# Chunked attention with a top-1 expert layer on one core: transposes in halves, a second score bank, and an early candidate list

## The chip, the cores and the metric

One core of a Trainium2 chip runs the whole kernel as one program. The metric is device time in microseconds (us); the median of the runs shown is the time of the kernel. The core's engines run their own instruction streams in order and wait for each other through semaphores: PE (matrix multiply, with its weight loads listed apart as PEld), DVE (vector), ACT (scalar, activations), POOL (general) and SP, which here only issues transfers. Transfers run on 16 DMA engines.

## The reference

`q`, `k`, `v` are 8 batches x 8 heads x 576 positions x 64. Attention is local to chunks of 64 positions. Its output, 4608 tokens x 512, goes through a gate that picks one of 8 experts per token; each expert keeps the 80 tokens with the highest gate weight, and all other rows of the output are zero.

```python
scores = scale * np.matmul(q_c, k_c.transpose(0, 1, 2, 4, 3))
scores = scores - np.max(scores, axis=-1, keepdims=True)
attn = np.exp(scores)
attn = attn / (np.sum(attn, axis=-1, keepdims=True) + 1e-09)
out = np.matmul(attn, v_c)
...
logits = x @ w_gate
expert_idx = np.argmax(logits, axis=1)
...
    if len(tok_idx) > capacity:
        gw = gate_w[tok_idx]
        keep = np.argpartition(-gw, capacity)[:capacity]
        tok_idx = tok_idx[keep]
    h = np.maximum(x[tok_idx] @ w1[e], 0.0)
    out[tok_idx] = gate_w[tok_idx, None] * (h @ w2[e])
```

## The kernel before

The 4608 tokens are 36 row tiles of 128 tokens (two chunks of 64, all 8 heads); four row tiles make one group. The program's text is the order of each engine's instructions, so an instruction that waits holds up everything written after it on its engine.

A loop over row tiles (iterations 0 to 34, the 36th written out behind it) is a pipeline of depth four. Iteration i makes, in this order: the scores of tile i (`scores`, 8 matmuls into `s`, on DVE a row maximum `mx` and the difference `sm`); on every fourth iteration the gate logits of an earlier group (`gate_mm`, `gate_copy`); for tile i-1 four transposes of `sm` into `pt` and an exponential on ACT (`probs`); for tile i-2 the values matmuls into `o` and the division on DVE, which gives `x` (`values`, which also stores x to memory through POOL); in gate iterations the gate's partial sums, four transposes `lT` (`gate_sum`); for tile i-3 four transposes of x into `px`, copied by ACT (`xtrans`); then SP issues the load of tile i-2+NB (`load`: q, and keys and values in two halves into one of NB buffers `kv`, whose unused places are zeroed once at the start). `s`, `pt` and `px` have one PSUM tile each.

A gate's DVE operations, and the steps of a search for each expert's threshold, stand in two queues, from which `fill` takes up to three between two DVE operations of the loop. The search brackets the threshold from the first 16 tiles; the rest of the loop and the tail count, for 256 levels inside the bracket, how many tokens lie above each level (`signs` on ACT or `steps_` on DVE make a level tile, `tally` sums them on PE into `ph`).

Weights of the first experts (EARLY) and zero writes of the output (CLEAR) are issued on SP in late iterations. After the loop the tail gates the last eight tiles, as two chains of four tiles whose steps alternate by the string LAST, finishes the counts, takes the exact threshold (`threshold`), masks all 36 tiles, numbers the kept tokens by a running sum (`inc`, `pos`, `ptok_b`), makes a one-hot matrix for each of the 36 tiles (`hot`, on DVE, ACT and POOL), and multiplies them into a list of up to 128 candidates (`cand`). These are ranked, and the 80 best rows per expert are gathered from memory (`xgc`). Then the experts' two matmul layers run, and the results are scattered to the output.

At the program's start DVE and POOL clear the seven buffers, and 14 matmuls on a zero tile (`warm`) run on PE ahead of the first scores.

## Time and profile before

| | |
|---|---|
| median of 3 runs | 275.99 us (274.03 to 277.04) |
| the profiled execution's own time | 273.62 us |
| its span | 271.4 us |
| PE busy | 246.6 us, 91% |
| PE weight loads (PEld) | 148.9 us, 55% |
| DVE busy | 134.7 us, 50% |
| ACT busy | 77.5 us, 29% |
| POOL busy | 55.2 us, 20% |
| transfers | 84.71 MB, mean 312 GB/s |

A row of single instructions or groups gives the start (us from the span's start), the duration, the engine, the line in the kernel, the operation, the tile written and the tiles read (numbers left out), the tile mode of PE (rows*columns), the shape (partitions x elements), the type and the count; brackets hold the idle time of the engine just before and what ended it. An fp32 matmul is two records, so four transposes are counted x8, of which some records can be missing. A row of a stretch of time gives start:end, its length, then busy time and instruction count of PE, PEld, DVE, ACT and POOL, the clock that PE was granted, the busy share of the DMA engines and their rate. A row of transfers gives the count, the size of one and the median time from issue to landing.

### The profile page before, as it was taken

How to read it: one execution, taken by the hardware profiler on the slowest of the kernel's cores; microseconds unless marked ns; L12 is line 12 of the kernel's file. 1: busy time of each engine (PE TensorE's matmuls, PEld its weight loads, DVE VectorE, ACT ScalarE, POOL GpSimd, SP SyncE). 2: the span in 40 equal slices, each digit the busy share in tenths (PEclk: the TensorE clock that was granted, in tenths of full speed). 3: DMA queues.
4: the chain of work that ended last, by engine and by line, in shares of the span. 5: the costliest groups of instructions: out<-in, count | busy, mean ns of one | idle time of the engine just before them, and what ended most of it. 6: DMA issues, size and time to landing. Idle time of an engine off the chain costs nothing. (4 is left out here: it accounts for less than half of the span.)

```text
span 271.4 us, 6612 instructions
## 1 busy us (share of the span) xinstructions
PE 246.6 (91%) x2703; PEld 148.9 (55%) x2703; DVE 134.7 (50%) x419; ACT 77.5 (29%) x159; POOL 55.2 (20%) x115
## 2 busy tenths in 40 slices
PE   0579999999999999999998878999999999999970
PEld 0458777777767687787876667342343434233320
DVE  7348758686767869695873867121121112112210
ACT  1003433433443554375755330220020202001000
POOL 9020101102020203069023453500000011110011
PEclk9999999999999999999999999999999999999996
DMA  4998799989998899979999971899999999996001
GB/s 145 381 282 294 250 323 386 347 280 315 390 341 315 278 342 318 378 261 391 395 408 408 331 297 44 295 368 406 404 393 408 407 403 393 407 387 244 0 36 35
DMA packets 32755, 84.71 MB, mean 312 GB/s; under 512 B 3344, under 2 KB 3472, under 8 KB 32720
## 3 DMA queue, kind: packets, MB, share of 16 engines
q1 hardware_dynamic: 28960, 71.32, 71.6%
q0 software_dynamic: 3456, 12.32, 13.0%
q10 hardware_dynamic: 304, 0.59, 0.6%
q8 instruction: 23, 0.38, 0.6%
q14 instruction: 12, 0.10, 0.1%
HBM read 64.04 MB, written 20.45 MB: 311 GB/s over the span
## 5 line engine op out<-in xcount | busy, mean ns | idle before, releaser
L202 PE MATMUL hc<-w,xtc 128*32 128x512 f32 x384 | 44.2, 594 | 0.2 <-ACT xtc L192 0.2
L235 PE MATMUL yc<-w,htc 128*32 128x512 f32 x384 | 43.4, 593 | 0.1
L316 PE MATMUL s<-kv,q 128*64 128x128 f32 x576 | 40.0, 282 | 1.8 <-POOL capc L768 1.7
L356 PE MATMUL o<-kv,pT 128*64 128x130 f32 x576 | 39.7, 279 | 0.0
L322 DVE TENSOR_REDUCE mx<-s 128x8 f32<-128x512 f32 x36 | 24.8, 690 | 22.4 <-PE s L316 22.3
L316 PEld LDWEIGHTS s<-kv,q 128*64 128x64 f32 x576 | 31.4, 138 | 8.3 <-issue 5.8
L356 PEld LDWEIGHTS o<-kv,pT 128*64 128x64 f32 x576 | 31.1, 135 | 5.9 <-issue 5.9
L338 ACT ACTIVATE pT<-pt 128x512 f32<-128x512 f32 x36 | 21.5, 597 | 35.1 <-PE pt L336 34.8
L235 PEld LDWEIGHTS yc<-w,htc 128*32 128x32 f32 x384 | 12.5, 110 | 29.2 <-issue 28.2
L202 PEld LDWEIGHTS hc<-w,xtc 128*32 128x32 f32 x384 | 12.1, 110 | 26.0 <-issue 25.6
L367 DVE TENSOR_TENSOR x<-o,rc 128x512 f32<-128x512 f32 x36 | 24.8, 689 | 0.8 <-DMA xs<-x 0.2
L325 DVE TENSOR_TENSOR sm<-s,mx 128x512 f32<-128x512 f32 x36 | 24.8, 690 | 0.6
L389 ACT COPY xT<-px 128x512 f32<-128x512 f32 x32 | 18.6, 581 | 22.1 <-PE px L388 22.0
L336 PE MATMUL pt<-ct,sm 128*128 128x128 f32 x144 | 23.5, 286 | 0.0
L388 PE MATMUL px<-ct,x 128*128 128x128 f32 x144 | 22.7, 283 | 0.8 <-ACT kv L389 0.8
L241 POOL DMA_INDIRECT out<-ysc,si x6 | 6.0, 995 | 84.8 <-DMA out<-zero 42.4
L207 ACT ACTIVATE hsc<-hc 128x512 f32<-128x512 f32 x6 | 3.6, 598 | 64.4 <-PE hc L202 64.4
L240 DVE TENSOR_SCALAR ysc<-yc,gatec 128x512 f32<-128x512 f32 x6 | 4.5, 752 | 34.5 <-PE yc L235 34.5
L336 PEld LDWEIGHTS pt<-ct,sm 128*128 128x128 f32 x144 | 15.1, 140 | 10.2 <-issue 9.5
L388 PEld LDWEIGHTS px<-ct,x 128*128 128x128 f32 x144 | 15.4, 141 | 5.1 <-issue 4.0
L463 POOL TENSOR_TENSOR comp<-comp,ct 128x32 bf16<-128x32 bf16 x18 | 3.9, 234 | 61.0 <-DVE comp L477 61.0
L209 DVE TENSOR_SCALAR hsc<-hc 128x512 f32<-128x512 f32 x6 | 4.1, 691 | 22.9 <-PE hc L202 22.9
(160 smaller groups left out, 242.3 us busy)
## 6 DMA issues: line engine op xcount, KB each, us to landing
w<-in_w SPq DMA_DIRECT2D x12, 2048.0 KB, 20.2
kv<-in_kv SPq DMA_DIRECT2D x70, 258.0 KB, 4.9
q<-in_q SPq DMA_DIRECT2D x36, 256.0 KB, 5.3
out<-zero SPq DMA_DIRECT2D x9, 1024.0 KB, 18.2
xs<-x POOLq DMA_DIRECT2D x8, 1024.0 KB, 7.1
w<-in_w SPq DMA_DIRECT2D x8, 1024.0 KB, 8.5
xs<-x POOLq DMA_DIRECT2D x4, 256.0 KB, 8.3
kv<-in_kv ACTq DMA_DIRECT2D x2, 258.0 KB, 4.2
```

The lines of the kernel that those rows point to most:

```text
L202: nc.tensor.matmul(h[o:o + 32, :], lhsT=xT[r][:, b, o:o + 32], rhs=getw(groups[r][g])[0][:, b, 512 * f:512 * f + 512], start=(b == 0), sto ...
L235: nc.tensor.matmul(y[o:o + 32, :], lhsT=hT[r][c // 4][:, c % 4, o:o + 32], rhs=getw(groups[r][g])[1][:, c, :], start=(c == 0), stop=(c == ...
L241: nc.gpsimd.indirect_dma_start(out=out, out_offset=bass.IndirectOffsetOnAxis(ap=si[:, r:r + 1], axis=0), in_=ys, in_offset=None, bounds_ch ...
L316: nc.tensor.matmul(ps[64 * u:64 * u + 64, pr, :].rearrange("p (h k) -> p h k", h=2), lhsT=t['q'][:, pr, u, :], rhs=t['k'][:, :, pr, u, :], ...
L322: nc.vector.tensor_reduce(mx, s8, axis=AX.X, op=ALU.max)
L325: nc.vector.tensor_tensor(sm.rearrange("p c k h -> p c h k"), s8, mx[:, :, :, None].to_broadcast([P, 4, 2, 64]), op=ALU.subtract)
L336: nc.tensor.transpose(pt[:, pr, :], sv[:, pr, :], ident)
L338: nc.scalar.activation(pT, pt, AF.Exp, scale=0.125)
L356: nc.tensor.matmul(po[64 * u:64 * u + 64, pr // 2, o:o + 130].rearrange("p (h x) -> p h x", h=2), lhsT=d['pT'][:, pr, 64 * u:64 * u + 64], ...
L367: nc.vector.tensor_tensor(t['x'][:, r, :].rearrange("p (j m e) -> p j m e", j=2, m=4), pov[..., 0:64], rc[:, :, :, None].to_broadcast([P, ...
L388: nc.tensor.transpose(pm[:, pr, :], t['x'][:, r, P * pr:P * pr + P], ident)
L389: nc.scalar.copy(t['xT'][:, :, P * r:P * r + P], pm)
```

## The change

- `halves` takes the place of the four transposes of 128 by 128 in `probs` and `xtrans`: eight of 64 rows by 64 columns, the two row halves of a pair into the two banks of one tile `tp`, shared by both callers. Two further places use `tp`, `s` and `o` for the last tiles.
- `s` gets two tiles. `values` of tile 34 writes two `s` tiles in place of one of two banks, and divides each by itself.
- The gate's partial sums are four matmuls against a constant of 8 columns (`summed`) in place of four transposes and a DVE reduction; the 1e-9 of the denominator is a constant ninth column of `ex`.
- NB goes from 7 to 6, NWARM from 14 to 24, and the start is written in another order.
- For the first R1 = 24 tiles the loop takes an early threshold from the counts so far (a level that the final one can't fall below), masks, numbers and positions them (`early_steps`, queued from LEVELS at 23), and makes the one-hots 12 to 23 on POOL (`early_hot`). From iteration 26 `fill` takes one step more.
- The tail gates the last eight tiles in one chain, multiplies the first 24 tiles into `cand1`, and then masks, numbers and picks only 12 tiles and one further column, which stands for the early list. `xtrans(32)` moves ahead of `probs(35)`.

```diff
-NB = 7
+NB = 6
...
-NWARM = 14
+NWARM = 24
...
-LEVELS = {15: "l0:4 c0 c1 c2 - - - - s2 c3", 19: "l4:5 - s3 s0 c4", 23: "l5:6 s4 s1 c5",
...
+LEVELS = {15: "l0:4 c0 c1 c2 - - - - s2 c3", 19: "l4:5 - s3 s0 c4", 23: "l5:6 s4 s1 - - t",
...
-LAST = "aaabababababababababab"
...
-HALVES = 32
-HOT = 8
+HOT = 12
+R1 = 24
+R2 = RT - R1
...
+            if S.get('hurry'):
+                step_one(bounds_q)
...
         def load(i):
+            load_q(i)
+            load_kv(i)
+
+        def load_q(i):
...
+
+        def load_kv(i):
+            T, r = divmod(i, 4)
+            kb = kvb[i % NB]
             for h in range(2):
                 (nc.scalar if i < 2 and h else nc.sync).dma_start(kb[h:P:2, h], kv[T, r, h])
...
-            ps = ps1.tile([P, 4, P], F32, name=f"s{i}", tag="s")
+            ps = ps1.tile([P, 4, P], F32, name=f"s{i}", tag="s", bufs=2)
...
+        def halves(src, nm, tag="tp"):
+
+            pm = ps1.tile([P, 2, 512], F32, name=nm, tag=tag)
+            for pr in range(4):
+                for u in range(2):
+                    rows = slice(64 * u, 64 * u + 64)
+                    nc.tensor.transpose(pm[:, u, 64 * pr:64 * pr + 64], src(pr)[rows],
+                                        ident[rows, rows])
+            return pm[:, :, 0:256].rearrange("p u (a j) -> p a u j", a=4)
...
             d = U[i]
-            pt = ps1.tile([P, 4, P], F32, name=f"pt{i}", tag="pt")
             sv = d['sm'].rearrange("p c k h -> p c (k h)")
-            for pr in range(4):
-                nc.tensor.transpose(pt[:, pr, :], sv[:, pr, :], ident)
+            pt = halves(lambda pr: sv[:, pr, :], f"pt{i}")
...
-            nc.scalar.activation(pT, pt, AF.Exp, scale=0.125)
+            nc.scalar.activation(pT.rearrange("p a (u j) -> p a u j", u=2), pt, AF.Exp,
+                                 scale=0.125)
...
+        def xtrans(i, tag="tp"):
             T, r = divmod(i, 4)
             t = TT[T]
-            if pm is None:
-                pm = ps1.tile([P, 4, P], F32, name=f"px{i}", tag="m")
+            dst = t['xT'][:, :, P * r:P * r + P]
+            if tag == "s":
+                pm = ps1.tile([P, 4, P], F32, name=f"px{i}", tag="s", bufs=2)
+                for pr in range(4):
+                    nc.tensor.transpose(pm[:, pr], t['x'][:, r, P * pr:P * pr + P], ident)
+            else:
+                pm = halves(lambda pr: t['x'][:, r, P * pr:P * pr + P], f"px{i}", tag)
+                dst = dst.rearrange("p a (u j) -> p a u j", u=2)
+            nc.scalar.copy(dst, pm)
...
+        def summed(lg, lt, n):
+            for c in range(n):
+                nc.tensor.matmul(lg[:, c, :], lhsT=lt[:, P * c:P * c + P],
+                                 rhs=ct[:, C_SUM:C_SUM + NE], start=True, stop=True)
...
+            lg = ps2.tile([P, n, NE], F32, name=f"lT{rt}", tag="g")
+            summed(lg, U[rt]['lt'], n)
             gate(rt, n, lg, gates)
...
+            if rt < 28:
+                fns[3:3] = [raised]
+            else:
+                w, ws, a = each("wi", inw)
+                o, os_, b = each("wl", nlo)
...
+                fns[6:6] = [w]
+                fns[8:8] = [o, ws, os_, lambda: v.tensor_tensor(bs, g, a, op=ALU.mult),
+                            lambda: v.tensor_tensor(bs, bs, b, op=ALU.add)]
...
+            def met():
+                S['ge1'] = gk.tile([P, 2, NE], BF16, name="ge1", tag="ge")
+                nc.vector.tensor_scalar(S['ge1'], left, 0.0, None, op0=ALU.is_le)
...
+            def pos1():
...
+                places(t, mask, inc)
...
+            def ptok1():
+                S['ptok_b'] = gk.tile([P, R1], BF16, name="ptok_b", tag="ptok_b", bufs=1)
+                place_of(S['ptok_b'], S['pos1'])
...
+            q = R1 - 4
+            for fn in ((signs, (q,)), (steps_, (nc.vector, q + 1)), (signs, (q + 2,)),
+                       (steps_, (nc.vector, q + 3)), wait, wait, wait, (left_add, (q, 4)),
+                       wait, wait, wait, (met, ()), wait, wait, wait, (met_pe, ()), wait, wait,
+                       (lambda: level(thr1, S['pn1']), ()),
+                       (above, (mask, 0, R1, thr1)), (running, (inc, mask, rst1)),
+                       wait, wait, wait, wait, (pos1, ()), wait, wait, wait, (ptok1, ())):
+                bounds_q.append(fn)
...
+        def early_hot():
+            if 'ptok' in S and pool_hots:
+                hot(pool_hots.popleft(), "p", 1)
...
-            for j, kb in enumerate(kvb):
-                (nc.vector if j % 2 == 0 else nc.gpsimd).memset(kb, 0.0)
-            load(0)
+            load_q(0)
             nc.scalar.dma_start(ident, cst[:, C_ID:C_ID + P])
             warm = gk.tile([P, 2 * P], BF16, name="warm", tag="lv", bufs=LV)
             nc.vector.memset(warm, 0.0)
+            for j, kb in enumerate(kvb):
+                if j:
+                    (nc.gpsimd, nc.vector)[j % 2].memset(kb, 0.0)
+                else:
+                    nc.vector.memset(kb[:, 0], 0.0)
+                    nc.gpsimd.memset(kb[:, 1], 0.0)
+            nc.vector.memset(wgp[:, :, 8:32], 0.0)
+            load_q(1)
+            load_kv(0)
...
             warm_up(NWARM)
...
-            for n in range(1, 4):
+            load_kv(1)
+            for n in range(2, 4):
...
+            for i in range(R1 + 4, RT - 1):
+                for h in (1, 2, 3):
+                    at(i, h, early_hot)
...
+                S['hurry'] = i >= R1 + 2
...
+            xtrans(32)
...
-            xtrans(32)
-            xtrans(33, ps1.tile([P, 4, P], F32, name="px33", tag="pt"))
-            px = ps1.tile([P, 2, 4, P], F32, name="px34", tag="s")
-            xtrans(34, px[:, 0])
-            xtrans(35, px[:, 1])
-            gate_mm(28, 4)
-            gate_mm(32, 4)
-            gate_copy(28, 4)
...
-            for w in LAST:
-                step_one(tails[w])
...
-            io_h = wk.tile([P, P, HOT], BF16, name="io_h", tag="x")
...
-            tally(32, 4)
+            hot(0, "v", HOT)
+            while pool_hots:
+                early_hot()
...
+            xtrans(33)
+            xtrans(34, "s")
+            two_logits(28, ps2, "g", "a", "sm")
+            xtrans(35, "o")
+            two_logits(30, ps2, "g", "v", "sm")
...
+            lg = ps2.tile([P, 8, NE], F32, name="lT28", tag="g")
+            for rt in (28, 30, 32, 34):
+                summed(lg[:, rt - 28:], lt[rt], 2)
+            gate(28, 8, lg, gates)
+            for j in range(len(gates) - 1):
+                step_one(gates)
...
+            for rt in range(R1):
+                nc.tensor.matmul(
+                    c1.rearrange("p c e -> p (c e)"), lhsT=S[rt],
+                    rhs=comp[:, rt].rearrange("p c e -> p (c e)"),
+                    start=rt == 0, stop=rt == R1 - 1)
...
+            tally(28, 8)
+            nc.vector.tensor_reduce(
+                kc1, c1[:, 2:5, :].rearrange("p c e -> p e c"), axis=AX.X, op=ALU.add)
+            nc.scalar.copy(cand1, c1)
...
-            mask = gk.tile([P, NE, RT], BF16, name="mask", tag="mask", bufs=1)
-            nc.vector.tensor_tensor(
-                mask, keys.rearrange("p r e -> p e r"),
-                thr[:, :, None].to_broadcast([P, NE, RT]), op=ALU.is_ge)
...
+            above(mask2[:, :, 1:], R1, RT, thr)
+            nc.vector.tensor_tensor(mask2[:, :, 0], kc1, thr, op=ALU.is_ge)
+            running(inc2, mask2, rst2)
...
+            place_of(ptok2[:, 0:R2], pos2[:, :, 1:])
...
-                n = 9 - len(others)
-                hot(b0, "v", n)
-                for j, way in enumerate(others):
-                    hot(b0 + n + j, way, 1)
-                order += range(b0, b0 + 9)
...
+            cand = two[1][:, 0:5 * NE].rearrange("p (c e) -> p c e", c=5)
+            half = (R2 + NE) // 2
+            for rt in (R1, R1 + half):
+                hot(rt, "v", half)
+            for rt in range(R1, RT):
                 nc.tensor.matmul(
                     cand.rearrange("p c e -> p (c e)"), lhsT=S[rt],
-                    rhs=comp[:, rt, 0:5].rearrange("p c e -> p (c e)"),
-                    start=rt == order[0], stop=rt == order[-1])
-                if rt % 9 == 8:
-                    keep_warm(4 if rt == order[-1] else 2)
+                    rhs=comp[:, rt].rearrange("p c e -> p (c e)"),
+                    start=rt == R1, stop=False)
+            for e in range(NE):
+                nc.tensor.matmul(cand[:, :, e], lhsT=S[RT + e], rhs=cand1[:, :, e],
+                                 start=False, stop=e == NE - 1)
+            keep_warm(4)
```

`places`, `place_of`, `above` and `running` hold the matmuls, the reduction, the comparison and the scan that stood in the tail. `each` makes a product with the one-hot of the expert and its sum over the experts.

On DVE, the program's start before: `kv` are the buffers of keys and values, `warm` is what the warm-up matmuls read, `wgp` the gate's weights, `mx` the first maximum.

```order
L738 MEMSET kv_103 128x2064
L738 MEMSET kv_105 128x2064
L738 MEMSET kv_107 128x2064
L738 MEMSET kv_109 128x2064
L742 MEMSET warm 128x128
L749 MEMSET wgp 128x4x24
L322 TENSOR_REDUCE mx_184<-s_175 128x8
```

The same place after the change:

```order
L851 MEMSET warm 128x128
L856 MEMSET kv_110 128x1032
L854 MEMSET kv_111 128x2064
L854 MEMSET kv_113 128x2064
L854 MEMSET kv_115 128x2064
L858 MEMSET wgp 128x4x24
L340 TENSOR_REDUCE mx_204<-s_195 128x8
```

The memset of `warm` moved from behind four buffers to the front, the first buffer is cleared here only by half, and three whole ones follow instead of four.

On PE, a gate iteration of the loop before, from the transposes of one iteration to the scores of the next; `L_0` are the gate logits, `ct` holds the identity.

```order
L388 MATMUL px_644<-ct,x_413 128x128 x4
L316 MATMUL s_654<-kv_107,q_434 64x128 x8
L400 MATMUL L_0_667<-xT_414,wgp 32x512 x4
L336 MATMUL pt_674<-ct,sm_620 128x128 x4
L356 MATMUL o_681<-kv_105,pT_627 64x130 x8
L421 MATMUL lT_694<-ct,lt_672 128x128 x4
L388 MATMUL px_707<-ct,x_629 128x128 x4
L316 MATMUL s_717<-kv_108,q_500 64x128 x8
```

After the change, where `ct` holds the sum constant too:

```order
L355 MATMUL px_484<-ct,x_264 128x64 x8
L334 MATMUL s_501<-kv_111,q_330 64x128 x8
L436 MATMUL L_514<-xT_265,wgp 32x512 x4
L355 MATMUL pt_521<-ct,sm_456 128x64 x8
L389 MATMUL o_532<-kv_115,pT_467 64x130 x8
L442 MATMUL lT_545<-ct,lt_519 128x8 x4
L355 MATMUL px_556<-ct,x_469 128x64 x8
L334 MATMUL s_570<-kv_112,q_381 64x128 x8
```

The blocks keep their sequence; `px` and `pt` are eight transposes of half the columns, and `lT` writes 8 columns instead of 128 per matmul.

On DVE, the tail from the threshold to the candidates' keys `kc` before; `pk` are one-hots.

```order
L667 SCALAR_TENSOR_TENSOR thr<-pn,step 128x8
L668 TENSOR_TENSOR thr<-thr,low 128x8
L861 TENSOR_TENSOR mask<-keys,thr 128x288
L866 SCALAR_TENSOR_TENSOR inc<-rst,mask 128x288
L877 TENSOR_REDUCE ptok_b<-two 128x36
L674 TENSOR_TENSOR pk_2478<-io_h,ptok_b 128x128x7
L674 TENSOR_TENSOR pk_2486<-io_h,ptok_b 128x128x7
L674 TENSOR_TENSOR pk_2494<-io_h,ptok_b 128x1024
L674 TENSOR_TENSOR pk_2500<-io_h,ptok_b 128x1024
L898 TENSOR_REDUCE kc<-two 128x8
```

After the change:

```order
L716 SCALAR_TENSOR_TENSOR thr<-pn,step 128x8
L717 TENSOR_TENSOR thr<-thr,low 128x8
L728 TENSOR_TENSOR mask_2780<-keys,thr 128x8x12
L999 TENSOR_TENSOR mask_2780<-kc_2721,thr 128x8
L733 SCALAR_TENSOR_TENSOR inc_2781<-rst_105,mask_2780 128x104
L742 TENSOR_REDUCE ptok_2796<-two_2785 128x12
L1009 CAST ptok_2796<-two_2785 128x8
L789 TENSOR_TENSOR pk_2799<-io_h,ptok_2796 128x128x10
L789 TENSOR_TENSOR pk_2801<-io_h,ptok_2796 128x128x10
L1026 TENSOR_REDUCE kc<-two_2786 128x8
```

Mask, scan and reduction run over 12 tiles and the added column in place of 36 tiles, and four one-hot operations for 30 tiles are two for 20 columns.

More of the change, by code (lines that the diff above doesn't have):

```diff
@@ L351, in values @@
             t = TT[T]
-            po = ps1.tile([P, 2, 512], F32, name=f"o{i}", tag="s" if last else "o")
+            if last:
+                po = [ps1.tile([P, 1, 512], F32, name=f"o{i}_{j}", tag="s", bufs=2)
+                      for j in range(2)]
+                bank, parts = (lambda j: po[j][:, 0]), [(slice(j, j + 1), po[j]) for j in range(2)]
+            else:
+                po = ps1.tile([P, 2, 512], F32, name=f"o{i}", tag="o")
+                bank, parts = (lambda j: po[:, j]), [(slice(0, 2), po)]
             for pr in range(4):
@@ new lines, in level, with threshold, above @@
+        def level(dst, pn):
+            nc.vector.scalar_tensor_tensor(dst, pn, 1.0, step, op0=ALU.max, op1=ALU.mult)
+            nc.vector.tensor_tensor(dst, dst, low, op=ALU.add)
+        def threshold():
+            ge = gk.tile([P, 2, NE], BF16, name="ge", tag="ge")
+            nc.vector.scalar_tensor_tensor(ge, U[28]['ph'], 0.5, left, op0=ALU.mult, op1=ALU.is_ge)
+            level(thr, levels_met(ge, "pn"))
+        fl = "p e r -> p (e r)"
+        def above(dst, r0, r1, t):
+            nc.vector.tensor_tensor(
+                dst, keys[:, r0:r1, :].rearrange("p r e -> p e r"),
+                t[:, :, None].to_broadcast([P, NE, r1 - r0]), op=ALU.is_ge)
@@ new lines, in running, with places, place_of @@
+        def running(dst, mask, reset):
+            nc.vector.tensor_tensor_scan(dst.rearrange(fl), reset.rearrange(fl),
+                                         mask.rearrange(fl), 0.0, op0=ALU.mult, op1=ALU.add)
+        def places(pos, mask, inc):
+            for j, (a, b) in enumerate(((tr_b, mask), (idp, mask), (ones_b, inc))):
+                nc.tensor.matmul(pos, lhsT=a, rhs=b.rearrange(fl), start=j == 0, stop=j == 2)
+        def place_of(dst, pos):
+            with nc.allow_low_precision(reason="whole numbers up to 256"):
+                nc.vector.tensor_reduce(
+                    dst, pos.rearrange("p e r -> p r e"), axis=AX.X, op=ALU.max)
@@ L868, in attention_moe @@
-            two = ps1.tile([P, 2, 512], F32, name="two", tag="s")
-            pos = two[:, 0, 0:NE * RT].rearrange("p (e r) -> p e r", e=NE)
-            for i, (a, b) in enumerate(((tr_b, mask), (idp, mask), (ones_b, inc))):
-                nc.tensor.matmul(pos.rearrange(fl), lhsT=a, rhs=b.rearrange(fl),
-                                 start=i == 0, stop=i == 2)
-            keep_warm(10)
-            ptok = S['ptok'] = gk.tile([P, RT], F32, name="ptok", tag="ptok", bufs=1)
-            ptok_b = S['ptok_b'] = gk.tile([P, RT], BF16, name="ptok_b", tag="ptok_b", bufs=1)
```

277 lines of the change are left out of this document (142 added, 135 removed).

## The prediction

> **What bounds the kernel now.** I cut the span by stages first: the wait for the first scores (s is the score tile), the start of the loop, the loop in two parts, and the tail up to the first expert work. Columns: busy time and instruction count of PE, PEld, DVE, ACT, POOL, then granted clock, DMA share, GB/s.
>
> ```profile
> core 0 of [0], span 271.4 us
> 0.00:12.78 12.78, 3.10 (x14) 1.94 (x15) 7.36 (x6) 1.79 (x3) 6.54 (x11) 1.00 0.72 255
> 12.78:28.02 15.24, 13.44 (x162) 10.80 (x161) 9.43 (x19) 2.98 (x5) 1.42 (x6) 1.00 0.91 298
> 28.02:88.75 60.73, 60.73 (x730) 45.76 (x729) 44.05 (x125) 23.90 (x44) 8.35 (x27) 1.00 0.94 327
> 88.75:138.56 49.81, 49.63 (x648) 37.96 (x647) 39.45 (x154) 27.58 (x63) 17.66 (x38) 1.00 0.94 342
> 138.56:169.20 30.64, 26.01 (x317) 20.44 (x316) 20.45 (x92) 10.76 (x26) 11.13 (x23) 1.00 0.79 292
> ```
>
> The loop (scores 5 to 35, 28.02 to 138.56) is PE's: it is busy throughout, DVE 44 of 61 us. Nothing but setup happens before 12.78. The timeline of the start says why:
>
> ```profile
> 1.24 1.78 DVE L738 MEMSET kv<- 128x2064 f32 x1 [1.24 <-PEq L1133]
> 3.04 0.58 SPq L307 DMA_DIRECT2D kv<-in_kv  x1
> ```
> ```profile
> 9.46 0.17 DVE L742 MEMSET warm<- 128x128 uint32 x1
> ```
> ```profile
> 9.68 3.17 PE L747 MATMUL pw<-warm 128*128 128x256 bf16 x14 [9.68 <-DVE warm L742]
> 12.78 1.69 PE L316 MATMUL s<-kv,q 128*64 128x128 f32 x16
> 16.14 1.09 PE L316 MATMUL s<-kv,q 128*64 128x128 f32 x16 [1.67 <-POOL capc L768]
> ```
> ```profile
> kv<-in_kv SPq DMA_DIRECT2D x1, 258.0 KB, 3.6
> ```
>
> Load 0 lands at 3.04 + 3.6 = 6.7, yet scores wait until 12.78, because the 14 warm-up matmuls stand ahead of them in PE's queue and wait for a memset that DVE runs after four others. Inside the loop, PE's rows of two iterations:
>
> ```profile
> 60.00 1.09 PE L316 MATMUL s<-kv,q 128*64 128x128 f32 x16
> 61.03 0.66 PE L336 MATMUL pt<-ct,sm 128*128 128x128 f32 x4
> 61.61 1.11 PE L356 MATMUL o<-kv,pT 128*64 128x130 f32 x16
> 62.65 0.66 PE L388 MATMUL px<-ct,x 128*128 128x128 f32 x4
> 63.24 1.09 PE L316 MATMUL s<-kv,q 128*64 128x128 f32 x16
> 64.26 1.06 PE L400 MATMUL L<-xT,wgp 128*32 128x512 f32 x8
> ...
> 66.88 0.66 PE L421 MATMUL lT<-ct,lt 128*128 128x128 f32 x4
> 67.37 0.27 PE L388 MATMUL px<-ct,x 128*128 128x128 f32 x1
> ```
>
> An iteration is 63.24 - 60.00 = 3.24 us, and a block of four transposes (pt, px) holds PE for 61.61 - 61.03 = 0.58.
>
> **The change, part by part.** *Start.* The warm memset comes first on DVE: 1.24 + 0.17 = 1.4. Fourteen warm-ups took 3.17, 0.23 each; 24 at that pace take 5.4 and end at 6.8. Buffer 0 is cleared in halves (0.9 each by the 1.78 row), so its load starts near 2.7 and lands at 6.3, under the warm-ups. Scores 0: 6.8 in place of 12.78. Scores 1 waited until 16.14 though both loads were there; the single score bank was being read (mx and sm, two DVE reads). With two banks only load 1 holds it: its memset ends near 4.9, and by the same 3.6, a little more behind load 0, it lands at 8.9. From there the iterations keep their spacing and the loads come at the DMA pace. Gain by scores 5: 16.14 - 8.9 = 7.2; bounds 5.5 and 7.5.
>
> *Half transposes.* How fast a transpose streams, and what half of one costs, stands in two places:
>
> ```profile
> 144.12 1.53 PE L388 MATMUL px<-ct,x 128*128 128x128 f32 x12
> ```
> ```profile
> 110.99 0.13 PEld L619 LDWEIGHTS pb<-ct,lo 64*128 64x128 f32 x1 [0.17 <-issue]
> 110.99 0.27 PE L619 MATMUL pb<-ct,lo 64*128 64x64 f32 x1
> 111.04 0.13 PEld L619 LDWEIGHTS pb<-ct,km 64*128 64x128 f32 x1
> 111.10 0.22 PE L619 MATMUL pb<-ct,km 64*128 64x64 f32 x1
> ```
>
> Twelve against four: (1.53 - 0.66) / 8 = 0.109 us a transpose. The 0.58 is then one weight load (0.05, the distance of the two pb loads), three steps of 0.109 and 0.20 until the next block, of another shape, starts. The pb rows are the new shape exactly, 64 rows by 64 columns, one after the other: a load every 0.05, and half the stream. If the halves on rows 0-63 and 64-127 run together, a block is 0.05 + 3 x 0.055 + 0.15 = 0.37 (minus 0.21); if in turn, 0.05 + 7 x 0.055 + 0.15 = 0.58 (nothing). The s rows show the kernel's column halves together: 16 matmuls of 128 columns in 1.03, 0.064 each against 0.109 alone. Nearest in kind, so I take minus 0.185, and 0.37 an iteration. No run here shows row halves together. [...]
>
> *Gate sums.* lT becomes matmuls with 8 columns, two records each: eight weight loads of 128 columns, at 0.055 to 0.109, and the next px is of another shape (0.1 more). From 0.49 (66.88 to 67.37) to 0.55 or 1.0; I take 1.0, plus 0.5 per gate. In return DVE drops two operations per gate, which costs nothing now.
>
> First loop part: 17 iterations, 4 gates: -17 x 0.37 + 4 x 0.5 = **-4.3** (ends -5.1 and +2), 56.4 of PE. DVE, with 44.05 busy in that stage, would be a near second and not yet the bound.
>
> *Second loop part.* The same terms give -13 x 0.37 + 3 x 0.5 = -3.3. Against it stand waits that no row of before shows; their parts are these:
>
> ```profile
> 46.77 0.69 DVE L322 TENSOR_REDUCE mx<-s 128x8 f32<-128x512 f32 x1 [0.38 <-PE s L316]
> ```
> ```profile
> 153.50 0.49 ACT L504 ACTIVATE lv<-io_b,bo 128x256 bf16<-128x256 bf16 x1
> ```
>
> At iteration 31 counts (ph) stand in PE's queue that wait for DVE's mx and a level tile behind it, an estimated 1.0; at 32 the early positions stand behind mx, sm (as long), mask and scan on DVE, while o covers 1.0: about 1.4; their matmuls 0.5; a dozen insertions between blocks of another shape, 0.1 each; two evictions of the shared transpose banks held up by a sign of 0.49, 1.0. Together +5.1, net **+2** (ends -3, all hidden, and +4).
>
> *Tail.* From the start of scores 35 (138.56) to the first gather:
>
> ```profile
> 149.61 0.29 DVE L425 TENSOR_REDUCE lg<-lT 128x32 f32<-128x128 f32 x1
> ...
> 153.14 0.18 DVE L499 TENSOR_REDUCE bo<-bv 128x4 f32<-128x32 f32 x1
> ...
> 155.55 0.67 DVE L861 TENSOR_TENSOR mask<-keys,thr 128x288 bf16<-128x288 f32 x1
> 156.25 0.76 DVE L866 TENSOR_TENSOR_SCAN inc<-rst,mask 128x288 bf16<-128x288 bf16 x1
> 157.38 0.46 DVE L877 TENSOR_REDUCE ptok_b<-two 128x36 bf16<-128x288 f32 x1 [0.37 <-PE two L871]
> 157.94 2.74 DVE L674 TENSOR_TENSOR pk<-io_h,ptok_b 128x896 bf16<-128x896 bf16 x4
> 162.78 0.18 DVE L898 TENSOR_REDUCE kc<-two 128x8 f32<-128x24 f32 x1 [2.09 <-PE two L889]
> ```
> ```profile
> 165.60 1.17 POOL L177 DMA_INDIRECT xgc<-xs,gic  x1 [3.94 <-DVE bt L906]
> ```
>
> Mask, scan and ptok shrink to 96 or 104 of 288 elements: 1.89 to about 0.9, -1.0. One-hots: 157.94 to 162.78 is 4.84; 20 columns at 2.74/30 are 1.8, and ten matmuls of the last half follow, 2.8 in all: -2.0. The gate chains, two interlaced, take 153.14 + 0.18 - 149.61 = 3.7; one chain of 13 operations at 0.2 (the 0.18 and a step) takes 2.6: -1.1. Longer gate sums +0.4. Three signs (0.49) before the eviction of px 32, partly under o, hold up pt 35: +0.7. The early one-hots run on POOL and DVE while PE does the last row tiles; the candidate matmuls of the first 24 wait for POOL, with the counts queued behind them, but the counts' own level tiles come later still. **-3** (ends -4.5 and +1).
>
> *Loads.* One buffer less: a load is issued four iterations ahead, 4 x 2.87 = 11.5 us, and the first took 3.6 to land. The loop would ask for 327 x 60.73/56.4 = 352 GB/s. The tenth after the loop moved 406:
>
> ```profile
> 140.00:150.00 10.00, 9.18 (x121) 6.83 (x119) 5.03 (x15) 4.29 (x9) 2.44 (x4) 1.00 1.04 406
> ```
>
> So I price it at nothing; without that cover, about +3, at the last loads, behind four weight transfers. The experts shift as a whole.
>
> **Sum.** -7.2 - 4.3 + 2 - 3 = -12.5. The profiled execution took 273.62 (span 271.4 and 2.2 around it), so 261.1; it lies 2.4 under the median of 275.99, from which the same sum gives 263.5. I say **262**.
>
> **The rivals.** *Halves in turn* (0.58 a block): 30 iterations x 0.37 lost, some of it under DVE's stalls, +9: 271. For: no row halves in the trace. Against: the s rows.
>
> *DMA and eviction take half of the loop's gain*: share 0.94 already, transpose banks shared: +5, 267.
>
> *The second part sticks*: ACT's signs and POOL's one-hots hold PE in every late iteration, 13 x 1.0: 275, no change. Against: ACT is busy 27.6 of 49.8.
>
> *Slower: weight loads set the pace.* Each half loads all 128 columns; if load and stream of the halves go in series, 0.109 a half, a block is 0.05 + 7 x 0.109 + 0.15 = 0.96, 0.38 over today's: 70 blocks, +27 on the 271, 298. It decides from 0.07 a half. Against: the pb loads are 0.05 apart. [...]
>
> **How the numbers follow.** Forecast 0.64, in turn 0.14, half lost 0.12, stuck 0.05, slower 0.05. The low end takes the better bounds (7.5, 0.21 a block, -1 in the second part, -4 in the tail): 257. The high end takes in halves in turn: 271. A measurement here tells about 1% (2.8 us). Faster: the first three, less their tails over 273.2, 0.87; within 0.07; slower 0.06.
>
> **What would show it.** Scores 0 near 7 and scores 1 near 9; a block of eight halves at 0.37 to 0.40 (0.58: in turn; 0.96: loads); the iteration at 2.87; lT near 1.0; PE waiting at ph of iteration 31 and the early positions; scores 35 near 128.5; two one-hot operations near 1 us; scores 35 to gather 24. Wrong would make it: scores waiting for loads, transposes waiting for ACT throughout, or a first gather much over 3.5 us because clears and weights still move.

## The result

The changed kernel takes 266.78 us (median of 4 runs, 265.45 to 267.74) against 276.51 for the kernel before beside it; the ratio is 0.966, with a 95% interval of 0.958 to 0.974. It is faster by 3.4%, where 4.2 to 5.1% was forecast (262 from a profiled execution of 273.62 and a median of 275.99). The time lies in the stated range, the sign and the main mechanism are as forecast, and the gain is smaller by a fifth to a third. Here and below a time is the median of all runs, and a ratio leaves out runs more than 1.5% above the fastest of their kernel.

The profiled execution of the changed kernel took 267.59 us, with a span of 265.8. The stretches that answer to those of the kernel before (same columns; the last one ends at the first expert work):

```profile
0.00:7.09 7.09, 4.06 (x24) 2.94 (x25) 4.96 (x5) 1.79 (x3) 6.38 (x18) 1.00 0.71 193
7.09:22.41 15.32, 14.10 (x185) 11.51 (x185) 10.71 (x20) 2.98 (x5) 1.46 (x7) 0.78 1.02 344
22.41:79.75 57.34, 56.91 (x886) 44.92 (x882) 43.66 (x120) 23.73 (x45) 9.03 (x30) 1.00 0.97 353
79.75:133.49 53.74, 49.23 (x765) 38.27 (x761) 40.31 (x155) 27.77 (x64) 20.11 (x41) 0.97 0.95 349
133.49:162.40 28.91, 25.86 (x348) 20.16 (x344) 18.47 (x85) 7.46 (x17) 10.51 (x21) 0.94 0.74 277
```

Three things are to be seen. The wait for the first scores went from 12.78 to 7.09 us. The first part of the loop is still PE's (56.91 of 57.34) and shorter by 3.4. The second part got longer, from 49.81 to 53.74, with 4.5 us in which PE is idle; before it was idle for 0.2. And the granted clock, the third value from the end, is under 1.00 in three stretches; it was 1.00 in all of them before.

A steady piece of the loop, PE's rows:

```profile
19.56 1.09 PE L334 MATMUL s<-kv,q 128*64 128x128 f32 x16
20.59 0.47 PE L355 MATMUL pt<-ct,sm 64*128 64x64 f32 x8
20.98 1.11 PE L389 MATMUL o<-kv,pT 128*64 128x130 f32 x16
22.02 0.46 PE L355 MATMUL px<-ct,x 64*128 64x64 f32 x8
22.41 0.44 PE L334 MATMUL s<-kv,q 128*64 128x128 f32 x4
```

In these rows a transpose is one record and any other fp32 matmul two, so x8 at pt and px are eight half transposes, as x4 before were four whole ones. A block of eight half transposes holds PE for 20.98 - 20.59 = 0.39 us in place of 0.58, and an iteration lasts 22.41 - 19.56 = 2.85 in place of 3.24. The forecast said 0.37 to 0.40 and 2.87.

The sum, term by term, from the two profiled executions (start: scores 5; the two parts of the loop; scores 35 to the first gather; the gather to the end of the span):

| | forecast | measured |
|---|---|---|
| start | -7.2 (-7.5 to -5.5) | -5.6 (28.02 to 22.41) |
| first part | -4.3 (-5.1 to +2) | -3.4 (60.73 to 57.34) |
| second part | +2 (-3 to +4) | +3.9 (49.81 to 53.74) |
| tail | -3 (-4.5 to +1) | -1.8 (27.04 to 25.27) |
| after the gather | 0 (up to +3) | +1.2 (105.8 to 107.05) |
| together | -12.5 | -5.6 of the span |

The medians differ by 9.7, not 5.6: the profiled execution of before (273.62) is quicker than all its timed runs (274.03 to 277.43), that of after one of the slower of its own. So of the 7 us missing in this table some 4 are a matter of which executions were profiled, and some 3 are missing from the gain.

### The profile page after: what moved, and what is told of

It is laid out like the page before. It is cut to its first block, busy times and chain, and to the rows that moved or that the text cites. A ratio compares the mean times of both kernels' runs of the same rounds, so it can differ in the third digit from the quotient of the medians.

```text
span 265.8 us, 7228 instructions
## 1 busy us (share of the span) xinstructions
PE 243.9 (92%) x3035; PEld 149.8 (56%) x3035; DVE 132.0 (50%) x407; ACT 74.2 (28%) x151; POOL 58.0 (22%) x124
## 4 chain that ended last, share of the span: by engine, by line
PE 70%; DMA 13%; DVE 9%; ACT 3%; issue 1%; POOL 0%; POOLq 0%; ACTq 0%
PE yc L237 13%; PE hc L204 12%; PE s L334 12%; PE o L389 11%; DMA w<-in_w 9%; PE pt L355 4%; PE px L355 4%; PE L L436 4%; PE lT L442 3%; DMA kv<-in_kv 2%; DVE mx L340 2%; PE hpc L222 2%; PE pwarm L805 2%; DMA xgc<-xs,gic 1%; DMA ct<-in_cst 1%; DVE sm L343 1%
## 5 line engine op out<-in xcount | busy, mean ns | idle before, releaser
L334 PE MATMUL s<-kv,q 128*64 128x128 f32 x576 | 41.1, 287 | 3.1 <-DMA kv<-in_kv 3.1
L334 PEld LDWEIGHTS s<-kv,q 128*64 128x64 f32 x576 | 32.3, 141 | 6.1 <-POOL rst L872 2.2
L237 PEld LDWEIGHTS yc<-w,htc 128*32 128x32 f32 x384 | 12.5, 110 | 30.0 <-issue 28.3
L405 DVE TENSOR_TENSOR x<-o,rc 128x512 f32<-128x512 f32 (+1 forms) x37 | 24.9, 675 | 0.9
L355 PEld LDWEIGHTS pt<-ct,sm 64*128 64x128 f32 x288 | 12.1, 142 | 13.2 <-issue 10.6
L355 PE MATMUL pt<-ct,sm 64*128 64x64 f32 x288 | 17.1, 240 | 1.7 <-ACT xT L430 1.0
L355 PE MATMUL px<-ct,x 64*128 64x64 f32 x280 | 16.1, 234 | 0.6 <-ACT pT L364 0.5
L501 POOL TENSOR_TENSOR comp<-mine,ct 128x32 bf16<-128x32 bf16 (+1 forms) x16 | 3.6, 243 | 53.5 <-DVE mine L515 42.0
L226 DVE COPY htc<-hpc 128x512 f32<-128x512 f32 x6 | 4.2, 692 | 22.0 <-PE hpc L222 22.0
```

The costliest lines, as they stand in the source:

```text
L237: nc.tensor.matmul(y[o:o + 32, :], lhsT=hT[r][c // 4][:, c % 4, o:o + 32], rhs=getw(groups[r][g])[1][:, c, :], start=(c == 0), stop=(c == ...
L334: nc.tensor.matmul(ps[64 * u:64 * u + 64, pr, :].rearrange("p (h k) -> p h k", h=2), lhsT=t['q'][:, pr, u, :], rhs=t['k'][:, :, pr, u, :], ...
L355: nc.tensor.transpose(pm[:, u, 64 * pr:64 * pr + 64], src(pr)[rows], ident[rows, rows])
L405: nc.vector.tensor_tensor(xv[:, js], pov[..., 0:64], rc[:, js, :, None].to_broadcast(w), op=ALU.mult)
```

## The experiments

The theory after the two traces: the halves are worth what the steady iteration shows; what is missing went to the halved clock, to gate sums that cost PE more than transposes, and to new waits of PE in the second part. The rival: another edit, the second score bank above all, made the loop shorter, and the halves need it. Ratios are to the kernel before, beside each run.

**Whole transposes again.** In the changed kernel:

```diff
-                for u in range(2):
-                    rows = slice(64 * u, 64 * u + 64)
-                    nc.tensor.transpose(pm[:, u, 64 * pr:64 * pr + 64], src(pr)[rows],
-                                        ident[rows, rows])
+                nc.tensor.transpose(pm[:, 0, P * pr:P * pr + P], src(pr), ident)
```

> The changed kernel with whole transposes again (four of 128 by 128 per block, still in the shared two-bank tile). If the halves are what shortened the loop, a block goes from 0.39 back to 0.58 us, the steady iteration from 2.85 to about 3.24, scores 5 to scores 22 from 57.3 to 63.8 us, and the time rises by 7 to 11 us, to 274 to 278. If instead the second score bank shortened the iteration, it stays near 2.85 and the time within 2 us of 266.8.

It took 277.12 us (10 runs), ratio 1.001 (0.995 to 1.006): no faster than the kernel before. A block is 0.59 again, and the first part of the loop, between scores 5 and 22, takes 63.4 in place of 57.3 us:

```profile
42.17 0.66 PE L353 MATMUL pt<-ct,sm 128*128 128x128 f32 x4
42.76 1.11 PE L386 MATMUL o<-kv,pT 128*64 128x130 f32 x16
```
```profile
23.08:86.46 63.38, 63.00 (x747) 47.77 (x746) 44.11 (x119) 24.23 (x45) 9.02 (x30) 1.00 0.92 318
```

Both score banks are in place here, so the halves alone carry the loop. And without them the rest of the change, the new start included, brings nothing: the loop is 7.5 us longer than in the kernel before (63.38 and 54.70 against 60.73 and 49.81), more than the 4.9 that scores 5 come earlier.

**The gates' partial sums by transposes again**, in the loop only:

```diff
-            lg = ps2.tile([P, n, NE], F32, name=f"lT{rt}", tag="g")
-            summed(lg, U[rt]['lt'], n)
+            lt = U[rt]['lt']
+            pm = ps2.tile([P, n, 4, 32], F32, name=f"lT{rt}", tag="g")
+            for c in range(n):
+                nc.tensor.transpose(pm[:, c].rearrange("p a b -> p (a b)"),
+                                    lt[:, P * c:P * c + P], ident)
+            lg = gk.tile([P, n, NE], F32, name=f"lg{rt}", tag="lg")
+            gates.append((lambda: nc.vector.tensor_reduce(
+                lg, pm[:, :, :, 0:8].rearrange("p c g e -> p c e g"), axis=AX.X, op=ALU.add), ()))
```

> The changed kernel with the gates' partial sums of the loop done by four transposes and a DVE reduction again, as before the change. If the eight weight loads of the sums cost what the trace shows (1.04 us a gate against 0.49), each of the seven gate iterations of the loop falls from 4.83 to about 4.3 and the time by 3 to 4 us, to about 263. It may also keep the clock up at iteration 31 (another 1.5), if it is the short matmuls of 8 columns that count as idle. If DVE is the bound there, the added reduction (0.29) takes the gain back: within 1 us of 266.8.

265.15 us, ratio 0.962 (0.954 to 0.970). The same place of a gate iteration, in the changed kernel first and then here:

```profile
31.55 1.06 PE L442 MATMUL lT<-ct,lt 128*128 128x8 f32 x8
32.54 0.46 PE L355 MATMUL px<-ct,x 64*128 64x64 f32 x8
```
```profile
32.34 0.66 PE L457 MATMUL lT<-ct,lt 128*128 128x128 f32 x4
32.92 0.46 PE L355 MATMUL px<-ct,x 64*128 64x64 f32 x8
```

Up to the next block it is 0.99 against 0.58, so the sums cost 0.41 a gate, and the gate iteration goes from 4.83 to 4.42; over seven gates of the loop that is 2.9 us. The first part of the loop gets 2.5 shorter (54.83). The whole loop takes 107.40, and 109.61 in the run with one score bank, whose clock stayed up in the loop as it did here: 2.2 less, while scores 35 wait 0.7 for a load here, so the 2.9 are there. The time falls by 1.6, less than the 3 to 4 expected and within the interval of the change itself. That the clock stayed up at iteration 31 tells nothing of the short matmuls: it stayed up too in two runs that kept them (fewer idle matmuls, one score bank).

**More warm-up**, so that PE isn't idle ahead of the scores:

```diff
-NWARM = 24
+NWARM = 42
...
                 scores(i)
+                if i == 0:
+                    warm_up(16)
```

> The changed kernel with 42 warm-up matmuls in place of 24, and 16 more behind the first scores, so that PE isn't idle from 5.1 to 7.1 and between the first two scores. If the halved clock from 7.1 to 13.9 us is what kept the start gain at 5.6 in place of 7.2, the first scores take 1.05 in place of 1.98, scores 2 start near 12.5 in place of 14.3 and scores 5 near 20.7 in place of 22.4: about 1.7 us less, 265. If the loads set the pace there (load 2 landed at 11.9, load 3 at 13.8, load 5 at 20.4), scores 5 stay within 0.5 of 22.4 and the time where it was.

266.07 us, ratio 0.963 (0.957 to 0.970). The clock stays up (1.00 in every microsecond up to 115), and scores 5 start at 21.78 in place of 22.41; but the warm-ups themselves now end late:

```profile
1.05 7.41 PE L865 MATMUL pw<-warm 128*128 128x256 bf16 x42 [1.05 <-DVE warm L851]
8.38 1.09 PE L334 MATMUL s<-kv,q 128*64 128x128 f32 x16
9.41 1.92 PE L865 MATMUL pw<-warm 128*128 128x256 bf16 x16
```

The scores take 1.09 in place of 1.98, as the clock theory said. From scores 1 to scores 5 it is 10.52 in place of 12.18, the whole 1.7 of the theory; but 0.6 of it comes out, since the first scores now wait for warm-ups instead of for loads (scores 1 start at 11.26 in place of 10.23).

**Fewer idle matmuls ahead of the last counts:**

```diff
-            keep_warm(18)
+            keep_warm(6)
             tally(28, 8)
```

> The changed kernel with 6 idle matmuls in place of 18 ahead of the last counts. They stand in PE's queue before the counts and ran at half clock from 146.9 to 150.7, while the last level tile was there at about 149.6. If they held up the counts, the gather comes 0.7 to 0.9 us earlier, about 266.0. If the counts wait for DVE or POOL anyway, nothing changes; if the clock stays down longer without them, the ranking behind it gets slower, up to 1 us the other way.

The stage does what was expected: the last counts no longer stand behind 3.79 us of idle matmuls but wait for level tiles themselves, and scores 35 to the gather falls from 25.27 to 24.42. The time is 267.15 us, ratio 0.966 (0.956 to 0.976): nothing that can be told from the changed kernel.

```profile
148.23 0.39 PE L569 MATMUL ph<-mine,lv 128*128 128x8 bf16 x3 [0.28 <-DVE lv L556]
```

**The halves alone**, in the kernel before (`halves`, `probs` and `xtrans` as in the change, the candidates' transposes in the shared tile):

```diff
+        def halves(src, nm, tag="tp"):
...
-            for pr in range(4):
-                nc.tensor.transpose(pt[:, pr, :], sv[:, pr, :], ident)
+            pt = halves(lambda pr: sv[:, pr, :], f"pt{i}")
...
-            nc.scalar.copy(t['xT'][:, :, P * r:P * r + P], pm)
+            nc.scalar.copy(dst, pm)
...
```

> The kernel before with one part of the change alone: the eight half transposes per block, for both callers through one two-bank tile. If the 0.385 us an iteration that the whole-transposes run gave back is the halves' own, scores 5 to 22 go from 60.7 to 54.2 and the second part from 49.8 to 45 to 47, and the time falls by 9 to 11.5, to 264 to 267, as much as the whole change gave. If the halves need the second score bank or the new order of gate steps beside them, the iteration stays over 3.0 and the time over 269.

268.65 us, ratio 0.979 (0.973 to 0.985): 2.1%, about half of what was expected. The stretch from scores 22 to 35 says where the rest went:

```profile
81.44:130.78 49.34, 45.97 (x754) 35.67 (x750) 39.38 (x157) 27.26 (x63) 17.60 (x38) 1.00 0.98 344
```

The first part is 6.0 shorter (54.74), as expected. In the second part PE has 3.7 us less work than before (45.97 against 49.63), and the stage is shorter by 0.5 only. In this kernel one transpose tile of two banks serves both callers (each half writes a bank of its own), and it makes PE wait for ACT, which is shown further down (3.2 us with start and halves); no run gave the halves of the two callers tiles of their own.

**The start alone**, in the kernel before:

```diff
-NWARM = 14
+NWARM = 24
...
-            for j, kb in enumerate(kvb):
-                (nc.vector if j % 2 == 0 else nc.gpsimd).memset(kb, 0.0)
-            load(0)
+            load_q(0)
...
             nc.vector.memset(warm, 0.0)
+            for j, kb in enumerate(kvb):
...
+            load_q(1)
+            load_kv(0)
...
```

> The kernel before with the new start alone: warm memset first, first buffer cleared in halves, loads 0 and 1 split, 24 warm-ups. Scores 0 near 7, scores 5 near 23 in place of 28.0; if the start's gain passes through to the end, the time falls by 4.5 to 5.5, to about 270.5. If the transfers, which then have 5 us less for the same bytes, set the end, less than 3 is left: 273.

268.93 us, ratio 0.980 (0.974 to 0.986): the start passes through to the end, with scores 5 at 23.35 and the loop as before (60.73 and 49.82). The rival, that transfers eat the gain, falls.

**One score bank in the loop:**

```diff
-            ps = ps1.tile([P, 4, P], F32, name=f"s{i}", tag="s", bufs=2)
+            ps = ps1.tile([P, 4, P], F32, name=f"s{i}", tag="s")
...
```

> The changed kernel with one score bank in the loop in place of two (the second bank stays for the last tiles). If the score bank is free in time once an iteration is in step (scores end 1.1 after their start, the two DVE reads take 1.4, the iteration 2.85), the steady iteration stays at 2.85 and only the start and the iterations with many DVE steps get longer: plus 0.5 to 2. If the second bank carries the loop, the iteration goes to 3.0 or more: plus 5.

266.25 us, ratio 0.970 (0.964 to 0.976): no difference from the changed kernel, and the iteration stays at 2.85. The second score bank does nothing that can be measured, at the start either: scores 1 start at 10.02 here and at 10.23 in the changed kernel.

**Without the early list**, the tail picks from all 36 tiles:

```diff
-            for rt in (R1, R1 + half):
-                hot(rt, "v", half)
+            for rt in (0, 12, 24):
+                hot(rt, "v", 12)
...
```

> The changed kernel without the early candidate list: no threshold, positions or one-hots for the first 24 tiles in the loop; the tail masks, numbers and picks all 36 tiles, with three one-hot operations of 12 columns on DVE. The tail then takes 2.0 to 3.0 us more (25.3 to about 28) and the loop's second part 2.0 to 3.5 less (53.7 to about 51). If the list's cost in the loop equals its gain in the tail, the time stays within 1 of 266.8; if the list pays by what the tail rows alone say, it rises by 2 to 3.

266.58 us, ratio 0.971 (0.964 to 0.977): no difference either.

```profile
78.20:128.85 50.65, 46.89 (x763) 37.27 (x761) 38.78 (x147) 29.56 (x67) 17.42 (x36) 1.00 0.97 350
128.85:156.71 27.86, 24.73 (x296) 19.22 (x297) 15.82 (x57) 6.03 (x13) 4.34 (x11) 0.88 0.83 316
```

The list saves 2.6 us in the tail (27.86 against 25.27, though two stretches at half clock fall into this tail and one into the changed kernel's). In the loop it costs 3.1 in the profiled executions (53.74 against 50.65); in executions of the changed kernel's loop whose clock stayed up (fewer idle matmuls, one score bank) the second part is 52.2, so 1.6 of the 3.1 is the clock. The other 1.5 is less than the list's steps take, for without them the loop runs into its loads. Scores 34 and 35 wait 1.8 us for keys and values:

```profile
124.13 1.09 PE L334 MATMUL s<-kv,q 128*64 128x128 f32 x16 [0.95 <-DMA kv<-in_kv]
128.85 1.09 PE L334 MATMUL s<-kv,q 128*64 128x128 f32 x16 [0.87 <-DMA kv<-in_kv]
```

By that sum, which is an estimate, the list holds up the loop for 3.3, and the loads hide 1.8 of what leaving it out would bring. NB is 6 here, as in the changed kernel.

**Start and halves together**, in the kernel before, and nothing else, with no edit beyond the two shown:

> The kernel before with the new start and the half transposes, and nothing else of the change. The start alone gave 5 to 6 us and the halves alone 5.6 to 7; if the two add up, the time is 11 to 12 below the kernel before, about 263.5, and so some 3 below the whole change: the rest of it (gate sums by matmul, second score bank, early list, one chain of gates) then costs more than it brings. If the two gains overlap (the transfers have 12 us less), 266 to 267, as the whole change.

263.89 us (6 runs), ratio 0.958 (0.954 to 0.963). The two gains add up (0.979 x 0.980 = 0.959), and two parts of the change do as well as all of it or better: 263.9 against 266.8, with intervals that overlap a little. What remains of PE's waits in the second part (the columns are total, times, longest):

```profile
PE px L345 <- ACT pT L354: 1.9, 2, 1.4
PE pt L345 <- ACT xT L409: 1.3, 2, 1.1
```

The kernel before has no such row. It kept `pt` and `px` in tiles of their own; now a transpose waits until ACT has emptied the other's. These 3.2 us are nearly all of PE's idle time there (49.33 less 45.96).

**The same with a longer warm-up:**

```diff
-NWARM = 24
+NWARM = 30
...
+                if i == 0:
+                    warm_up(16)
```

> The same with 30 warm-up matmuls in place of 24 and 16 more behind the first scores, so that PE has work until load 1 is there. If idle time of PE in the first 10 us is what halves its clock there, scores 5 start near 21.5 in every run and the time falls by another 1, to about 262.5; if not, nothing changes.

262.44 us, ratio 0.953 (0.949 to 0.958), scores 5 at 21.34 in place of 23.72. The step is as large as expected; its interval overlaps that of the run before it.

**The whole change with its three costs taken out** (sums by transposes, 6 idle matmuls, the longer warm-up), edits as above:

> The whole change, with its gate sums by transposes and a DVE reduction again, 6 idle matmuls ahead of the last counts in place of 18, and the same warm-ups (30 and 16). By the single runs: 1.6 for the sums, 0.8 for the counts, 0.7 for the start, 263.5 in all if they add up. If the early list is then still paid for in the loop, it stays level with the kernel that has only start and halves; if the list is a net gain once the sums don't slow the loop, it lies 1 or more below it.

263.88 us, ratio 0.959 (0.954 to 0.964): level with the kernel that has only start and halves, and 1.4 behind the one that has the longer warm-up too, with intervals that overlap. The early list is paid for in two places:

```profile
76.63:129.41 52.78, 46.62 (x755) 36.03 (x752) 41.75 (x163) 28.07 (x64) 20.46 (x45) 1.00 0.95 340
129.41:154.00 24.59, 21.80 (x291) 16.89 (x292) 14.91 (x61) 7.42 (x17) 9.04 (x19) 0.86 0.96 357
```
```profile
L237 PE MATMUL yc<-w,htc 128*32 128x512 f32 x384 | 43.4, 593 | 1.9 <-DMA w<-in_w 1.9
```

The tail is 3.1 shorter than with start and halves alone (24.59 against 27.71), the second part 3.45 longer (52.78 against 49.33), and now the second expert layer waits 1.9 us for weights, which it did for 0.2 there. Something else is in the 3.45: scores wait 1.0 for a load in this part (and 0.6 in the first). Such waits inside the loop show in three runs, all with NB at 6 (this one, the one without the list, the one with the sums by transposes), and in none with NB at 7, though the loop is shorter there (104.07 with start and halves alone, 108.24 here). That it is the missing buffer is argued from this alone; no run put the seventh buffer back into the changed kernel.

**Search counts apart, wide one-hots**, on the kernel with start, halves and the longer warm-up:

```diff
-                for j in range(2):
+                for j in range(3):
+                    bounds_q.extend([wait] * (1, 5, 0)[j])
                     bounds_q.append((search_count, (i, j)))
-                bounds_q.extend([wait] * 7)
+                bounds_q.extend([wait] * 3)
...
-            for b0, others in ((0, "ap"), (9, "ap"), (18, "a"), (27, "p")):
+            for b0 in (0, 12, 24):
+                hot(b0, "v", HOT)
```

> The kernel with start, halves and the longer warm-up (262.4), with two more edits that the trace tells apart by stage. In the loop, the two sign counts of a search step on ACT (0.7 each with its readout) no longer stand next to each other, and start one step after the bounds they wait for. If it is such a count ahead of an eviction on ACT that holds PE through the shared transpose tile (3.2 us of PE waits on ACT in the second part, 1.4 the longest), the wait of 1.4 at iteration 24 goes and the second part falls from 50.4 (with a clock dip of 1.5) to 47.5 to 48; if DVE's own queue is behind it, the wait only moves and the stage stays at 49. In the tail, three one-hot operations of 12 columns on DVE take the place of 30 columns in four and six single ones on ACT and POOL: first one-hot to candidates' keys 3.7 (as in the kernel without the early list) in place of 4.8. Together 260 to 260.5; 262.4 if neither holds.

261.55 us, ratio 0.952 (0.949 to 0.956). It is the fastest of all, by an amount that can't be told from the run it builds on. The wait of 1.4 is gone, but others came, of PE for DVE, and the stage is 48.70 against 49.33 (the run with a full clock there):

```profile
PE pt L345 <- ACT xT L409: 0.8, 1, 0.8
PE pc L599 <- DVE rc L382: 0.7, 1, 0.7
PE pc L599 <- DVE gg L500: 0.7, 1, 0.7
```

So "the wait only moves" holds for most of it. The one-hots do about what was expected, 149.51 - 145.57 = 3.9 from the first to the keys in place of 4.8:

```profile
145.57 2.70 DVE L694 TENSOR_TENSOR pk<-io_h,ptok_b 128x1536 bf16<-128x1536 bf16 x3
149.51 0.18 DVE L924 TENSOR_REDUCE kc<-two 128x8 f32<-128x24 f32 x1 [1.24 <-PE two L915]
```

Yet the tail as a whole did not get shorter (28.27 against 27.94): what stands ahead of the one-hots took 0.6 longer, and so did what lies between the keys and the gather, which was not followed further.

## Why the prediction was right, and where it fell short

**Bound and mechanism: right.** PE sets the loop; the halves on rows 0-63 and 64-127 run together: in the steady block above the two of a pair start less than 0.01 us apart, the second pair 0.11 after the first and the others 0.06 apart, close to the 0.064 of the scores' column halves. The choice of 0.185 a block, nearest those column halves, came out at 0.19. (The 16 of the scores are two records each of 8 matmuls, so the likeness was closer in number than in kind.) The rivals "halves in turn" (0.58) and "weight loads set the pace" (0.96) fall by the measured 0.39.

**Start: mis-sized, -5.6 for -7.2.** Two steps failed. The first is "twenty-four at that pace take 5.4 and end at 6.8". They took 4.06. The pace did not hold: up to 3.6 us one warm-up starts 0.21 after the other, from 3.7 on 0.11. The count of warm-ups running in each microsecond of the changed kernel shows it (one that runs across a border counts in both; PE's time and count in each stretch, then clock, DMA share, GB/s), while the clock column reads 1.00 for both paces:

```profile
2.00:3.00 1.00, 1.00 (x7) 1.00 0.69 188
3.00:4.00 1.00, 1.00 (x8) 1.00 1.14 386
4.00:5.00 1.00, 1.00 (x11) 1.00 1.00 279
```

So PE stood idle from 5.11 until load 0 was there, and its granted clock was 0.50 from 7.1 to 13.9, over both first scores:

```profile
7.09 1.98 PE L334 MATMUL s<-kv,q 128*64 128x128 f32 x16 [1.99 <-DMA kv<-in_kv]
10.23 1.97 PE L334 MATMUL s<-kv,q 128*64 128x128 f32 x16 [1.16 <-DMA kv<-in_kv]
```

The second step is "the same 3.6" for the loads: load 0 landed at 7.0 and load 1 at 10.1, 4.9 and 5.8 after their issue. In the kernel before, the load issued next, at 4.55, already landed 4.05 later. So scores 1 started at 10.23 for 8.9, and that is 1.3 of the missing 1.6; from there to scores 5 it took 12.18, where the sum kept the 11.88 of before.

What the halved clock costs shows between profiles. With new start and halves, scores 5 start at 20.84 to 21.78 in the six whose clock stays up after the warm-ups, and at 22.41 to 23.72 in the four where it is halved; from scores 1 on, which leaves out when load 1 landed, it is 10.5 to 11.7 against 12.2 to 13.3. Two of the six have the same 24 warm-ups (one score bank, without the early list), with gains of 6.9 and 7.2. So the forecast size was within reach: with 24 warm-ups the clock stayed up in two profiles and was halved in four, with the longer warm-up it stayed up in all four. What decides it with 24 was not shown.

**First part: -3.4 for -4.3.** Halves and gates came as forecast (2.85 and 4.83, from 2.87 and 4.80). The rest is a stall of 0.9 in iteration 21, where the search takes its keys; before, those matmuls stood in iteration 22, in the second part, and PE did not wait at them.

**Second part: the sign of the term was right, its size wrong, +3.9 for +2.** The longest waits of PE in this stretch (total, times, longest), then two rows of iteration 31:

```profile
PE pt L355 <- ACT xT L430: 1.0, 3, 0.5
PE pos L738 <- DVE inc L733: 0.7, 1, 0.7
PE ph L569 <- DVE lv L556: 0.6, 1, 0.6
PE pn L712 <- DVE ge L754: 0.6, 1, 0.6
```
```profile
116.26 1.92 PE L436 MATMUL L<-xT,wgp 128*32 128x512 f32 x8
...
118.73 1.58 PE L389 MATMUL o<-kv,pT 128*64 128x130 f32 x16
```

The waits at the counts (ph), at the early positions (pos) and for ACT are where they were said to be, 0.6, 0.7 and 1.0 for forecasts of 1.0, 1.4 and 1.0. The wait for the early level (pn, 0.6) was not foreseen, and logits and values ran at half clock (1.92 for 1.06, 1.58 for 1.11). That made iteration 31 last 8.4 us; in the run with fewer idle matmuls, where the clock stayed up there, it is 6.8. No row of before could show these 1.6 us.

**Tail: -1.8 for -3.** By parts, from lines of the changed kernel's DVE:

```profile
146.06 0.23 DVE L511 TENSOR_REDUCE gm<-lT 128x8 f32<-128x64 f32 x1 [1.36 <-PE lT L442]
...
148.19 0.17 DVE L528 TENSOR_TENSOR bo<-bo,wls 128x8 f32<-128x8 f32 x1
...
152.10 0.32 DVE L728 TENSOR_TENSOR mask<-keys,thr 128x96 bf16<-128x96 f32 x1
...
153.52 1.56 DVE L789 TENSOR_TENSOR pk<-io_h,ptok 128x1280 bf16<-128x1280 bf16 x2
155.94 0.18 DVE L1026 TENSOR_REDUCE kc<-two 128x8 f32<-128x24 f32 x1 [0.85 <-PE two L1020]
```

Mask to one-hots: 1.42 for 2.39, the forecast 1.0 less. One-hots to keys: 2.42 for 4.84, 2.4 less (forecast 2.0). One chain of gates: 2.3 for 3.7, 1.4 less (forecast 1.1). What the sum left out stands between the last bo and the mask: 3.7 us in place of 2.2. All eight level tiles are made there after one chain, and the counts, at 150.51, stood behind 18 idle matmuls that ran at half clock; with 6 of them 0.85 came back.

```profile
146.88 3.79 PE L805 MATMUL pwarm<-io_b,ones_b 128*128 128x256 bf16 x18
```

The chain's gain was thus given back one step later. Scores 35 to the first gate operation took 12.6 for 11.05, 1.5 more where 1.1 was priced.

**Loads and experts: +1.2 for 0.** With one buffer less the loop of the changed kernel never waited for a load, as said; it did, for 0.7 to 1.8 us, in three of the runs whose loop was made shorter, so "I price it at nothing" held only as long as the loop was slow. "The experts shift as a whole" failed by 0.7: the second layer's matmuls waited 0.8 for weights (0.1 before). The gather came 6.8 us earlier, the last weights landed 5.6 earlier (244.6 for 250.25). The other 0.5 was not followed.

The rivals "DMA and eviction take half" and "the second part sticks" each hold a piece: evictions through the shared tile hold up PE, but only in the second part (1.0 us at pt, 0.5 at px; no such wait in the first), where ACT has extra work, and the late iterations stick, for 4.5 us of idle PE in all, not for 1.0 in each of 13. The prediction priced what is added to the second part at +5.1 against -3 in the tail, and the gate sums at +0.5 each; it did not draw from that that start and halves alone might be the better kernel.

## What to carry to other kernels

Cost a change of many edits one by one and look for the subset: here two edits carry the whole gain (0.958 against 0.966 with all), and the others trade tail for loop. A faster block on the bound engine is worth its full size only where nothing else stands close behind it; the halves gave 6.0 us in the loop's even part and 0.5 in the part where ACT and DVE have extra steps, since sharing one transpose tile made PE wait for ACT (3.2 us of that part with start and halves). And a cover that is enough for a slow loop, here six buffers, has to be counted again when the loop gets faster (0.7 to 1.8 us of waits for loads in three runs here). The halves write two banks, one for each row half; no run tried them in one.

## What was not expected of the hardware

In the changed kernel's profile the granted clock of PE changes on a grid. It is one half from 7.10 to 13.92, 116.32 to 119.74 and 147.04 to 150.46 us:

```profile
112.91:116.32 3.41, 2.79 (x64) 2.33 (x68) 3.02 (x12) 1.50 (x4) 2.10 (x7) 1.00 1.04 416
116.32:119.74 3.42, 3.42 (x27) 1.64 (x28) 0.30 (x2) 1.18 (x2) 0.00 (x0) 0.50 1.02 403
123.15:126.56 3.41, 2.41 (x41) 1.71 (x35) 3.02 (x12) 0.83 (x2) 0.00 (x0) 1.00 1.05 408
143.63:147.04 3.41, 3.41 (x50) 2.98 (x47) 1.30 (x5) 0.26 (x1) 2.19 (x4) 1.00 1.02 340
```

The dips last one or two times 3.41 us and lie whole multiples of it apart (13.92 to 116.32 is 30 of them); a last one, from 259.7 to the end, comes after PE's last matmul. When a dip comes differs between executions: iteration 31 had one here and none in the run with fewer idle matmuls, and the first warm-ups sped up anywhere from 3.7 to 6.8 us after the start of the span (ten profiles).

Idle time of PE does not tell by itself where the clock falls. Ahead of the first dip PE stood idle for 1.99 us, but the stretch ahead of the second has PE busy for 2.79 of 3.41 us, that ahead of the third for all of it, while 2.41 from 123.15 on is followed by no dip. So busy time in the profile alone is not what the clock goes by. Both stretches ahead of the second and third dip hold many matmuls of 8 or 40 columns (ph and lT, cand); whether they have to do with it was not tried. In the loop one dip makes the second part 1.6 longer (53.74 and 53.76 with it, 52.18 and 52.19 without, in four executions of the same loop, one of them with one score bank), more than several of the edits here are worth.
